# A recurrence with an expert layer behind it: the same steps issued in another order, with other transposes on the DMA queue

## The chip, the cores and the metric

The kernel runs on one core of a Trainium2 chip. The metric is the time of one execution on the device in microseconds (us); lower is better. The engines are named as the profile names them: PE is TensorE (PEld its weight loads), DVE is VectorE, ACT is ScalarE, POOL is GpSimd, and SP is SyncE, whose queue issues nearly all DMAs here. Each engine takes its instructions in the order in which they were issued to it, and an instruction that waits holds up all behind it.

## The reference

Thirty-two heads (batch 4, 8 heads) of width 40 carry a state over 768 steps; the outputs of all heads of a token form a row of 320, and a layer with 2048 hidden units follows. Cut to what matters:

```python
for t in range(S):
    y[:, :, t] = np.einsum('bhd,bhde->bhe', rt, state)
    Sa = np.einsum('bhde,bhe->bhd', state, at)
    state_decay = state * wt[:, :, None, :] - np.einsum('bhd,bhe->bhde', Sa, bt)
    state = state_decay + np.einsum('bhd,bhe->bhde', vt, kt)
...
x = attn_out.transpose(0, 2, 1, 3).reshape(B * S, H * D)
h = x @ w_in                      # 3072 x 320 @ 320 x 2048
g = np.maximum(h, 0.0) ** 2
return g @ w_out                  # 3072 x 2048 @ 2048 x 320
```

## The kernel before

The 768 steps are cut into 12 chunks of 64. Within a chunk the recurrence is written as matrix products over the chunk's steps, for 16 pairs of heads; from chunk to chunk only the state is handed on. The names of the steps carry the chunk's number `c`:

- Loads: `ldw`, `ldk`, `ldb`, `lda`, `ldr`, `ldv c` bring the six inputs into the tiles `raw_w`, `raw_kb`, `raw_a`, `raw_r`, `raw_v`, two buffers of each. A load is two DMAs of 160 KB (`ldw` four of 80 KB in chunks 0 to 3). `lwi`, `lwl` and `lwo` bring the expert weights, through tiles that later hold other data.
- Preparation: `ln` (logarithm of w, tile `lnW`), `hi` and `lo` (its two halves), `cf` and `ci` (running sums, on PE), `eg`, `ef`, `ec`, `ei`, `ex` (exponentials, tiles `iG`, `GT`, `Gin`), `castk`, `castb`, `castA`, `castR`, `castV` (to bf16) or `mulKB` (keys times `iG`, from chunk 4).
- Transposes on PE and their evictions: `Tk`, `Tb`, `TK` to `KBT`; `TA`, `TR` to `AR`; `TU` back from `KBT`; `TV` to `VUT`; `TS` to `Sb`; `XT` to `XT`. The eviction has the same name in small letters. A transpose is either narrow (two matmuls of 64 rows each per block) or wide (one matmul of 128 rows), as the table `WIDE` says.
- Transposing DMAs: for chunks in `TV_DMA`, `TS_DMA`, `TK_DMA` the transpose of V, of the state or of K is no step of PE but a DMA on SyncE's queue, `ldt`, `lds` or `ldz`.
- The chain from chunk to chunk: `EN` and `mEN` (products of keys, masked on DVE), `AS` (the old state's part), `EV`, `u0`, `NU`, `u1` (the corrected values, tile `VU`), `S` and `s` (the new state `STb`).
- The output of a chunk: `CX`, `mCX`, `RS`, `Y`, `y`, `yd`, `XT`, `xt`.
- The expert layer: `F` and `FL` (first product, units u0 to u3; `FL` is the last 64 rows of the input width), `f` (maximum with 0), `q` (square), `O` (second product; `OL` for chunk 11), `o` (eviction), `st` (store).
- `WD` steps are matmuls whose result nobody reads.

PE writes into four PSUM tiles `pb`, and a step that opens one names it (`PE2` is the third); it waits until what was there has been evicted.

A planner has written out what is issued when: its string `ORDER` names an engine and a step in each entry, and `Plan.issue` goes through it from first to last. A step can have several possible engines (copies may go to DVE, ACT or POOL), and the entry says which. The engines run by themselves after that, held only by data, buffers and semaphores. DMAs take eight semaphores in turn: a DMA can be issued only when the last one with the same semaphore has landed, so no more than eight are under way.

Of the kernel before, what the change touches and what calls it, by code (L numbers as in the profile page):

```python
# [88 lines left out]
1; DVE hi 0 h1; DVE zs 1; POOL zk 1; POOL castk 0; DVE lo 0 h1; PE cf 0 h1; ACT eg 0 h0; POOL
castb 0; ACT eg 0 h1; DVE zk 0; SP lda 0; PE1 Tk 0; DVE za 0; DVE tk 0 g1; DVE tk 0 g0; PE3 Tb 0;  # L90
DVE tb 0 g0; ACT ef 0; DVE tb 0 g1; PE2 ci 0 h0; PE ci 0 h1; POOL castA 0; PE0 TA 0; DVE tA 0 g1;
PE1 WD2; POOL zk 2; PE1 TU 0; SP ldw 1; ACT ln 1; ACT ec 0; DVE tA 0 g0; DVE tU 0; PE3 EN 0 g1;
DVE mEN 0 g1; POOL hi 1; SP ldk 1; PE0 EN 0 g0; POOL lo 1; ACT ldb 1; ACT castA 1; SP ldv 0; PE2
cf 1; PE1 TA 1; POOL castV 0 g1; ACT eg 1; POOL castV 0 g0; ACT ef 1; DVE mEN 0 g0; PE3 ci 1; ACT
ec 1; SP ldw 2; DVE tA 1 g1; PE0 EV 0; POOL castk 1; PE2 Tk 1; ACT u0 0; PE NU 0; ACT ln 2; DVE tA
1 g0; ACT u1 0 g0; ACT u1 0 g1; DVE tk 1 g0; DVE tk 1 g1; POOL castb 1; PE1 Tb 1; DVE tb 1 g0; SP
ldr 0; POOL castR 0; DVE tb 1 g1; PE3 TR 0; ACT tR 0 g1; POOL hi 2; ACT tR 0 g0; PE2 S 0 g0; PE S
0 g1; DVE s 0 q0; SP ldv 1; DVE s 0 q1; PE0 TV 0; ACT tV 0; POOL lo 2; ACT castV 1 g1; PE1 EN 1
g1; DVE mEN 1 g1; SP ldb 2; PE3 EN 1 g0; DVE mEN 1 g0; PE2 TU 1; ACT tU 1; PE0 CX 0 g1; DVE mCX 0
g1; PE1 cf 2; SP ldv 2; POOL zv 1; SP lda 2; PE3 CX 0 g0; PE2 AS 1; POOL castV 1 g0; PE EV 1; DVE  # L100
mCX 0 g0; POOL castb 2; PE0 Tb 2; ACT eg 2; POOL castA 2; DVE tb 2 g1; ACT u0 1; DVE tb 2 g0; PE3
TA 2; PE NU 1; ACT ef 2; DVE tA 2 g0; SP ldk 2; PE1 Y 0; DVE yd 0; DVE y 0; DVE tA 2 g1; SP ldr 1;
POOL castR 1; SP lwi 0 u1; POOL cwi 0 u1; ACT u1 1 g0; ACT u1 1 g1; PE0 SC 1; PE S 1 g0; SP lwi 0
u0; PE S 1 g1; DVE s 1 q0; ACT castk 2; PE1 XT 0; PE2 ci 2; ACT castV 2 g1; ACT xt 0; ACT ec 2;
PE3 Tk 2; DVE s 1 q1; PE1 TR 1; ACT tR 1 g0; ACT tR 1 g1; PE2 TV 1; DVE tk 2 g0; PE0 EN 2 g0; DVE
tk 2 g1; PE3 EN 2 g1; DVE mEN 2 g0; SP ldw 3; POOL castV 2 g0; ACT tV 1; POOL zv 2; ACT ln 3; POOL
hi 3; DVE mEN 2 g1; PE1 TU 2; SP lwl 0; DVE tU 2; POOL lo 3; PE0 TS 1; DVE tS 1; SP ldr 2; POOL
castR 2; SP ldk 3; SP ldb 3; PE2 AS 2; PE EV 2; PE3 TS 0; SP lwi 0 u2; PE1 CX 1 g1; DVE tS 0; ACT
u0 2; ACT cwl 0; PE NU 2; ACT u1 2 g0; DVE mCX 1 g1; PE0 CX 1 g0; DVE mCX 1 g0; ACT u1 2 g1; PE3
cf 3; ACT ef 3; PE1 SC 2; PE S 2 g0; PE S 2 g1; POOL castk 3; PE2 F 0 u1; PE0 Tk 3; DVE s 2 q1;  # L110
POOL cwi 0 u0; ACT eg 3; DVE s 2 q0; ACT castb 3; DVE tk 3 g0; SP lda 3; PE FL 0 u1; ACT f 0 u1;
DVE tk 3 g1; PE3 ci 3; ACT ec 3; SP ldv 3; PE1 RS 1; PE Y 1; PE2 TV 2; ACT tV 2; PE3 FL 0 u2; DVE
y 1; DVE yd 1; PE1 XT 1; PE0 Tb 3; DVE xt 1; DVE tb 3 g0; POOL cwi 0 u2; DVE tb 3 g1; PE F 0 u2;
ACT f 0 u2; POOL castA 3; PE1 TA 3; SP lwi 0 u3; PE2 TR 2; ACT tR 2 g0; ACT tR 2 g1; DVE tA 3 g0;
ACT castV 3 g1; DVE tA 3 g1; PE0 TS 2; POOL cwi 0 u3; PE3 F 1 u1; DVE tS 2; PE FL 1 u1; ACT f 1
u1; SP ldw 4; SP lwo 0 x3; POOL castV 3 g0; ACT ln 4; PE2 CX 2 g1; POOL cwo 0 x3; PE1 FL 0 u3; DVE
mCX 2 g1; SP ldb 4; PE0 EN 3 g1; POOL hi 4; POOL lo 4; SP ldr 3; POOL castR 3; PE F 0 u3; DVE mEN
3 g1; POOL q 1 u1; PE3 F 1 u0; PE2 EN 3 g0; DVE mEN 3 g0; ACT f 0 u3; PE0 CX 2 g0; DVE mCX 2 g0;
ACT q 0 u3; PE FL 1 u0; ACT f 1 u0; PE1 FL 1 u2; SP lwo 0 x0; POOL cwo 0 x0; PE F 1 u2; PE2 F 0
u0; PE FL 0 u0; DVE f 0 u0; POOL q 0 u0; PE3 ci 4 h0; ACT f 1 u2; SP lwo 0 x1; ACT ex 4 h0 g1; PE0  # L120
cf 4; PE1 AS 3; PE EV 3; POOL cwo 0 x1; DVE u0 3; ACT ef 4; PE2 RS 2; PE Y 2; ACT ei 4 h0; SP lda
4; ACT ex 4 h0 g0; SP lwo 0 x2; PE0 ci 4 h1; ACT ex 4 h1 g1; DVE y 2; POOL q 0 u1; PE NU 3; ACT ei
4 h1; ACT u1 3 g0; SP lwo 0 x5; POOL cwo 0 x5; PE3 FL 1 u3; DVE yd 2; PE2 TU 3; DVE tU 3; DVE u1 3
g1; SP lwo 0 x4; PE F 1 u3; ACT ex 4 h1 g0; PE0 TR 3; ACT castA 4; SP lwo 0 x6; PE2 TA 4; DVE tA 4
g0; DVE tA 4 g1; ACT f 1 u3; PE1 SC 3; PE S 3 g0; PE S 3 g1; DVE s 3 q0; DVE s 3 q1; PE3 TV 3; ACT
q 0 u2; SP ldw 5; SP lwo 0 x7; PE2 O 0 u0; ACT q 1 u0; DVE tR 3 g0; POOL cwo 0 x2; DVE tR 3 g1; PE
O 0 u1; ACT tV 3; PE1 CX 3 g0; ACT ln 5; ACT cwo 0 x7; PE3 TS 3; PE0 XT 2; ACT xt 2; POOL cwo 0
x6; DVE tS 3; DVE mCX 3 g0; POOL z 3; ACT k 3 q0; SP ldk 4; SP ldr 4; POOL cwo 0 x4; PE O 0 u2; PE
O 0 u3; DVE o 0; PE1 CX 3 g1; POOL hi 5; POOL lo 5; PE0 ci 5 h1; ACT q 1 u3; PE3 FL 2 u0; POOL
mulKB 4 h1; ACT ex 5 h1 g1; PE F 2 u0; POOL mulKB 4 h0; POOL q 1 u2; ACT ex 5 h1 g0; ACT ei 5 h1;  # L130
# [1067 lines left out]
```

## Time and profile before

| what | us |
| --- | --- |
| three runs | 236.6, 236.7, 237.03 |
| median | 236.7 |
| the profiled execution | 236.31 |
| its span, first to last instruction | 234.4 |

The granted TensorE clock was 0.993 of full speed over the span. The span can be read in three parts. Until the first expert product on PE the chunks 0 to 2 are loaded and prepared, and so are the expert weights. Then PE works on the recurrence and the expert layer in turn, and loads and transposing DMAs go on beside it. In the last part the recurrence is done and the expert products of chunks 10 and 11 follow each other.

In rows of the profile, `out<-in` are tiles of the kernel, `xN` is the number of instructions in a row, and what stands in brackets at the end is how long the engine was idle before it and what ended that.

### The profile page before, as it was taken

How to read it: one execution, taken by the hardware profiler on the slowest of the kernel's cores; microseconds unless marked ns; L12 is line 12 of the kernel's file. 1: busy time of each engine (PE TensorE's matmuls, PEld its weight loads, DVE VectorE, ACT ScalarE, POOL GpSimd, SP SyncE). 2: the span in 40 equal slices, each digit the busy share in tenths (PEclk: the TensorE clock that was granted, in tenths of full speed). 3: DMA queues.
4: the chain of work that ended last, by engine and by line, in shares of the span. 5: the costliest groups of instructions: out<-in, count | busy, mean ns of one | idle time of the engine just before them, and what ended most of it. 6: DMA issues, size and time to landing. Idle time of an engine off the chain costs nothing.

```text
span 234.4 us, 11927 instructions
## 1 busy us (share of the span) xinstructions
PE 221.3 (94%) x5367; PEld 172.0 (73%) x5367; DVE 179.4 (77%) x228; ACT 176.1 (75%) x235; POOL 141.6 (60%) x144
## 2 busy tenths in 40 slices
PE   8768979998999999999999999997999999999997
PEld 2558868786887677787788687775677877878873
DVE  5777999887687768978987878969689677758550
ACT  3467997978997969799888988986789933863631
POOL 7659326446999774379774959682296990320320
PEclk9997999999999999999999999999999999999999
DMA  6899697997997888887889799799999796811004
GB/s 167 230 193 196 187 243 196 239 184 163 312 213 148 158 156 203 160 151 156 196 179 178 152 171 174 145 183 167 195 120 175 154 165 142 170 37 47 12 6 108
DMA packets 115609, 38.26 MB, mean 163 GB/s; under 512 B 99690, under 2 KB 115558, under 8 KB 115558
## 3 DMA queue, kind: packets, MB, share of 16 engines
q1 hardware_dynamic: 114006, 36.19, 76.3%
q10 hardware_dynamic: 1552, 1.31, 2.0%
q8 instruction: 42, 0.69, 1.2%
q14 instruction: 9, 0.07, 0.1%
HBM read 28.84 MB, written 3.93 MB: 140 GB/s over the span
## 4 chain that ended last, share of the span: by engine, by line
PE 66%; DMA 13%; SPq 6%; ACT 5%; POOL 4%; issue 3%; DVE 2%; POOLq 0%; ACTq 0%; DVEq 0%
PE pb L391 37%; PE pb L987 22%; DMA G<-in_moe_w_in_dram 5%; PE pb L395 4%; DMA raw_w<-in_w_dram 3%; DMA VUT<-VU 2%; DMA raw_kb<-in_k_dram 2%; PE pb L399 2%; ACT G L1015 2%; SPq L434 2%; SPq L464 1%; SPq L1101 1%; PE pb L1153 1%; POOL WIN L381 1%; ACT Gin L670 1%
## 5 line engine op out<-in xcount | busy, mean ns | idle before, releaser
L1023 POOL TENSOR_TENSOR G<-G 128x1024 bf16<-128x1024 bf16 x25 | 47.2, 1893 | 29.0 <-DVE G L1017 14.6
L391 PE MATMUL pb<-WOUT,G 128*128 128x320 bf16 x384 | 56.2, 299 | 0.1
L987 PE MATMUL pb<-XT,WIN 128*128 128x256 bf16 x384 | 48.4, 273 | 0.5 <-ACT G L1015 0.3
L391 PEld LDWEIGHTS <-G 128*128 128x128 bf16 x384 | 36.3, 98 | 14.5 <-issue 0.7
L1015 ACT ACTIVATE G<-pb 128x1024 bf16<-128x1024 f32 x36 | 36.5, 1022 | 10.3 <-PE pb L987 9.0
L987 PEld LDWEIGHTS <-WIN 128*128 128x128 bf16 x384 | 34.9, 98 | 7.9 <-issue 3.2
L765 DVE TENSOR_TENSOR CX<-pb,UTI 128x1024 bf16<-128x1024 f32 x24 | 28.8, 1218 | 6.9 <-PE pb L391 5.2
L765 DVE TENSOR_TENSOR EN<-pb,MSK 128x1024 bf16<-128x1024 f32 x24 | 28.8, 1218 | 3.3 <-PE pb L391 3.0
L385 POOL TENSOR_TENSOR KB<-raw_kb,iG 128x640 bf16<-128x640 f32 x13 | 19.9, 1543 | 11.1 <-ACT iG L664 5.3
L1025 ACT ACTIVATE G<-G 128x1024 bf16<-128x1024 bf16 x19 | 19.8, 1054 | 3.5 <-DVE G L1017 3.3
L1017 DVE TENSOR_SCALAR G<-pb 128x1024 bf16<-128x1024 f32 x12 | 14.6, 1220 | 6.7 <-PE pb L987 5.1
L866 DVE TENSOR_TENSOR STb<-pb,GT 40x640 bf16<-40x640 f32 x22 | 18.1, 822 | 1.5 <-PE pb L391 1.1
L740 DVE TENSOR_TENSOR AR<-pb,GT 128x512 bf16<-128x512 bf16 x24 | 15.7, 683 | 4.1 <-PE pb L395 2.4
L987 PE MATMUL pb<-XT,WLAST 64*128 64x256 bf16 x192 | 17.2, 271 | 1.1 <-ACT G L1015 0.9
L391 PEld LDWEIGHTS <-EN 64*64 64x64 bf16 (+1 forms) x768 | 14.7, 111 | 3.7 <-issue 2.9
L385 POOL TENSOR_TENSOR lo<-lnW,hi 128x640 bf16<-128x640 f32 (+1 forms) x11 | 14.8, 1347 | 3.0 <-PE pb L391 2.3
L949 DVE TENSOR_TENSOR Yb<-pb,Gin 128x128 bf16<-128x128 f32 (+1 forms) x24 | 12.3, 549 | 3.3 <-PE pb L391 3.3
L670 ACT ACTIVATE Gin<-pb 64x320 f32<-64x320 f32 x32 | 13.7, 429 | 1.0 <-PE pb L391 0.4
L377 ACT ACTIVATE VU<-pb 64x640 bf16<-64x640 f32 x18 | 12.5, 696 | 1.8 <-issue 1.1
L377 ACT ACTIVATE VUT<-pb 128x2048 bf16<-128x2048 bf16 x6 | 11.2, 1874 | 2.7 <-PE pb L395 1.9
L377 ACT ACTIVATE osb<-pb 128x640 f32<-128x640 f32 (+1 forms) x8 | 5.1, 636 | 10.8 <-PE pb L391 10.8
L701 ACT ACTIVATE GT<-pb 128x1024 f32<-128x1024 f32 x12 | 12.3, 1021 | 0.7 <-PE pb L391 0.6
(127 smaller groups left out, 443.9 us busy)
## 6 DMA issues: line engine op xcount, KB each, us to landing
raw_kb<-in_k_dram SPq DMA_DIRECT2D x24, 160.0 KB, 4.3
raw_v<-in_v_dram SPq DMA_DIRECT2D x24, 160.0 KB, 4.8
raw_a<-in_a_dram SPq DMA_DIRECT2D x22, 160.0 KB, 3.2
raw_r<-in_r_dram SPq DMA_DIRECT2D x22, 160.0 KB, 4.5
out_dram<-osb SPq DMA_DIRECT2D x22, 160.0 KB, 2.7
raw_kb<-in_b_dram SPq DMA_DIRECT2D x20, 160.0 KB, 4.9
G<-in_moe_w_in_dram SPq DMA_DIRECT2D x10, 256.0 KB
raw_w<-in_w_dram SPq DMA_DIRECT2D x16, 160.0 KB, 5.1
```

The costliest lines, as they stand in the source:

```text
L377: alts.append(("ACT", c_act(n), lambda: nc.scalar.activation(out=o_(), in_=i_(), func=ACTF.Copy, scale=1.0 if scale is None else scale)))
L385: return [("POOL", 40 + 2.35 * n, lambda: nc.gpsimd.tensor_tensor(out=o_(), in0=a_(), in1=b_(), op=op)), ("DVE", c_dve(n), lambda: nc.vect ...
L391: return lambda: nc.tensor.matmul(out=o_(), lhsT=l_(), rhs=r_(), start=start, stop=stop, skip_group_check=True)
L670: nc.scalar.activation(out=Gin[c % NGI][rows(g), NP * jh:NP * jh + NP, :].rearrange("p j e -> p (j e)"), in_=slot(hb, FP32)[rows(g), g, 0: ...
L740: ew(f"tA {c} g{g}", [("DVE", c_dve(512), lambda g=g: nc.vector.tensor_tensor(out=steps(AR[q2][:, 0, g]), in0=turned(ha, g), in1=steps(GT[ ...
L765: ew(f"m{nm} {c} g{g}", [("DVE", c_dve(1024), lambda: nc.vector.tensor_tensor(out=dst[q2][:, g].rearrange("p q i t -> p (q i) t"), in0=slo ...
L866: ew(f"s {c} q{q}", [("DVE", c_dve(2 * n), lambda q=q: nc.vector.tensor_tensor(out=STb[q2][live(q), :, q, 0:D], in0=slot(hs, FP32)[live(q) ...
L987: return lambda: nc.tensor.matmul(out=o_(), lhsT=l_(), rhs=r_(), start=begins and opens(hf, x), stop=ends and not opens(hf, x), skip_group ...
L1015: ("ACT", c_act(1024), lambda gb=gb, hf=hf: nc.scalar.activation(out=gb, in_=slot(hf, FP32)[:], func=ACTF.Relu)),
L1017: ("DVE", c_dve(1024), lambda gb=gb, hf=hf: nc.vector.tensor_scalar(out=gb, in0=slot(hf, FP32)[:], scalar1=0.0, scalar2=None, op0=ALU.max))],
L1023: ("POOL", 1900, lambda gv=gv: nc.gpsimd.tensor_tensor(out=gv, in0=gv, in1=gv, op=ALU.mult)),
L1025: ("ACT", c_act(1024), lambda gv=gv: nc.scalar.activation(out=gv, in_=gv, func=ACTF.Square))],
```

## The change

The kernel's code stays, and so do the steps. The tables and the string `ORDER` change:

- `TV_DMA` loses chunk 8, `TS_DMA` gains chunk 5, `TK_DMA` gains chunk 9: nine transposing DMAs become ten, and PE has `TV 8` for `TS 5` and `TK 9`.
- `WIDE`: `Tk 1`, `Tb 2`, `Tk 3`, `TA 3`, `TR 3`, `TA 4`, `TR 8`, `TR 9`, `TV 2`, `TV 3` become narrow; `TA 0`, `TR 2`, `TR 6`, `TV 1` become wide. (`cf 4` and `cf 7` in it have no effect.)
- `ORDER` puts the steps into another order on all engines, and some 130 evictions, casts, squares and the like on another engine. `WD` steps: 2 at the start and 11 at the end before; 7 at the start and 8 at the end now. The expert products of chunk 0 and 1 begin in it ahead of most of chunk 3's steps.

```diff
-TV_DMA = (8, 9, 10, )
-TS_DMA = (6, 8, 9, 10, )
-TK_DMA = (10, 11, )
-WIDE = """TA 1; TA 3; TA 4; TR 0; TR 1; TR 3; TR 8; TR 9; TS 1; TU 0; TU 1; TU 2; TU 3; TV 2; TV 3; Tb 0;
-Tb 1; Tb 2; Tk 0; Tk 1; Tk 2; Tk 3"""
+TV_DMA = (9, 10, )
+TS_DMA = (5, 6, 8, 9, 10, )
+TK_DMA = (9, 10, 11, )
+WIDE = """TA 0; TA 1; TR 0; TR 1; TR 2; TR 6; TS 1; TU 0; TU 1; TU 2; TU 3; TV 1; Tb 0; Tb 1; Tk 0; Tk 2;
+cf 4; cf 7"""
...
-ORDER = """ACT ldw 0 h1; SP ldw 0 h0; DVE zs 0; DVE zr 0; ACT ldb 0; DVE zz 0; DVE zr 1; SP ldk 0; POOL za 1;
+ORDER = """POOL zv 0; DVE zk 1; SP ldw 0 h0; POOL zr 0; DVE zs 1; DVE zr 1; ACT ldw 0 h1; DVE zs 0; ACT ldk 1;
...
```

Three places show what moves. In the rows the line numbers are those of each kernel (the new one's code stands three lines higher), and a number behind a tile's name tells its buffer.

ScalarE in the first third of the start, before: `ln 1`, the load b 1 (`raw_kb_68`), then the preparation of chunk 1, `u0 0` (`NZ`), `ln 2` (`lnW` from `raw_w_65`) and `u1 0` (`VU`).

```order
L615 ACTIVATE lnW_75<-raw_w_66 128x640
L647 ACTIVATE Gin_79<-pb_151 128x640
L449 DMA raw_kb_68<-in_b_dram 128x1x320 x2
L377 ACTIVATE tA_91<-raw_a_70 128x2x8x40
L566 ACTIVATE iG_78<-pb_151 128x1024
L701 ACTIVATE GT_83<-pb_151 128x16x64
L647 ACTIVATE Gin_80<-pb_152 128x640
L377 ACTIVATE NZ_94<-pb_149 128x640
L615 ACTIVATE lnW_75<-raw_w_65 128x640
L377 ACTIVATE VU_87<-pb_149 64x16x40 x2
```

The same stretch now:

```order
L612 ACTIVATE lnW_75<-raw_w_66 128x640 [waits DMAHW5_49,DMAHW6_49,DMAHW2_49,DMAHW7_49,DVE_49,Activation_49]
L461 DMA raw_a_70<-in_a_dram 128x1x320
L461 DMA raw_a_70<-in_a_dram 128x1x320 [waits DMAHW3_49]
L446 DMA raw_kb_67<-in_k_dram 128x1x320 [waits DMAHW4_49,DMAHW0_49,Pool_49]
L446 DMA raw_kb_67<-in_k_dram 128x1x320 [waits DMAHW1_49]
L644 ACTIVATE Gin_80<-pb_150 128x640 [waits PE_49]
L563 ACTIVATE iG_78<-pb_151 128x1024 [waits DVE_49,PE_49,Activation_49]
L698 ACTIVATE GT_83<-pb_151 128x16x64
L374 ACTIVATE NZ_94<-pb_152 128x640 [waits DVE_49,PE_49]
L612 ACTIVATE lnW_75<-raw_w_65 128x640 [waits DMAHW1_49,DMAHW2_49,DMAHW0_49,DMAHW3_49,Activation_49,Pool_49]
L374 ACTIVATE VU_87<-pb_152 64x16x40 [waits PE_49]
```

The loads a 1 (`raw_a_70`) and k 2 (`raw_kb_67`) now stand on ScalarE's queue behind `ln 1`, and the load of a 0 and of k 1 ahead of it; `ln 2` still stands between `u0 0` and `u1 0`.

SyncE's queue from the load w 2 (`raw_w_65`, four DMAs) to v 1 (`raw_v_74`), before, with what each DMA waits for:

```order
L434 DMA raw_w_65<-in_w_dram 32x8x80 [waits DMAHW6_49,Activation_49]
L434 DMA raw_w_65<-in_w_dram 32x8x80 [waits DMAHW7_49,DMAHW3_49]
L434 DMA raw_w_65<-in_w_dram 32x8x80 [waits DMAHW0_49]
L434 DMA raw_w_65<-in_w_dram 32x8x80 [waits DMAHW1_49]
L474 DMA raw_r_71<-in_r_dram 128x1x320 [waits DMAHW2_49]
L474 DMA raw_r_71<-in_r_dram 128x1x320 [waits DMAHW3_49]
L458 DMA raw_v_74<-in_v_dram 64x16x40 [waits DMAHW4_49]
L458 DMA raw_v_74<-in_v_dram 64x16x40 [waits DMAHW5_49]
```

And now:

```order
L431 DMA raw_w_65<-in_w_dram 32x8x80 [waits DMAHW0_49,Activation_49]
L431 DMA raw_w_65<-in_w_dram 32x8x80 [waits DMAHW3_49,DMAHW1_49]
L431 DMA raw_w_65<-in_w_dram 32x8x80 [waits DMAHW2_49]
L431 DMA raw_w_65<-in_w_dram 32x8x80 [waits DMAHW3_49]
L471 DMA raw_r_71<-in_r_dram 128x1x320 [waits DMAHW4_49]
L471 DMA raw_r_71<-in_r_dram 128x1x320 [waits DMAHW5_49]
L455 DMA raw_v_74<-in_v_dram 64x16x40 [waits DMAHW6_49]
L455 DMA raw_v_74<-in_v_dram 64x16x40 [waits DMAHW7_49]
```

The rows are the same; what stands behind the semaphores is not. In the new program the semaphores 2 and 3 belong to the load a 1 at that point, and 4 and 5 to the load k 2, both on ScalarE's queue; the third and fourth DMA of w 2 and the load r 0 wait for those.

SyncE's queue near two thirds of the program, where a transposing DMA was late before:

```order
L452 DMA raw_kb0_67<-in_k_dram 64x16x40 x2
L1058 DMA out_0_dram<-osb0_115 64x2x320 x2
L458 DMA raw_v1_74<-in_v_dram 64x16x40 x2
L909 DMA_TRANSPOSE VUT0_97<-VU2_89 128x16x128
L464 DMA raw_a0_69<-in_a_dram 128x1x320 x2
L885 DMA_TRANSPOSE Sb0_107<-STb0_105 128x16x128
```

And now:

```order
L1055 DMA out_0_dram<-osb0_115 64x2x320 x2
L435 DMA raw_w1_66<-in_w_dram 64x16x40 x2
L538 DMA_TRANSPOSE KBT1_96<-KB0_84 128x16x128
L449 DMA raw_kb0_67<-in_k_dram 64x16x40 x2
L461 DMA raw_a0_69<-in_a_dram 128x1x320 x2
L1055 DMA out_0_dram<-osb0_115 64x2x320 x2
```

`ldt 8` (to `VUT`) is gone, since `TV 8` is a step of PE now, and `ldz 9` (to `KBT`) stands near its place.

More of the change, by code (lines that the diff above doesn't have):

```diff
@@ L89 @@
[L89 to L130, printed above, removed]
```

217 lines of the change are left out of this document (128 added, 89 removed).

## The prediction

> **What bounds the kernel now.** I read the page first, then the waits of TensorE, then stretches of 5 us, and last the order of time on ScalarE's, SyncE's and TensorE's own queues. The page says that PE is busy nearly throughout:
>
> ```profile
> span 234.4 us, 11927 instructions
> ...
> PE 221.3 (94%) x5367; PEld 172.0 (73%) x5367; DVE 179.4 (77%) x228; ACT 176.1 (75%) x235; POOL 141.6 (60%) x144
> ```
>
> The chain of waits has PE's first expert product at 43 us; from there to 230 us PE's waits for others are nearly one single wait:
>
> ```profile
> 43.19 0.98 PE pb L987 x8
> ```
>
> ```profile
> PE pb L391 <- DMA VUT<-VU: 2.0, 1, 2.0
> PE pb L987 <- ACT G L1015: 1.2, 2, 0.9
> ```
>
> So after 43 us an order can gain through PE's own work, through that 2.0 us, and through short handoffs of a PSUM bank. Ahead of 43 us it is different. Three stretches (busy time of each engine, granted clock, DMA share, GB/s):
>
> ```profile
> 5.00:10.00 5.00, 4.05 (x54) 2.44 (x53) 2.83 (x7) 2.13 (x6) 3.79 (x6) 1.00 0.96 259
> 15.00:20.00 5.00, 3.34 (x101) 2.65 (x96) 2.81 (x4) 3.78 (x5) 3.38 (x5) 1.00 0.87 178
> 20.00:25.00 5.00, 4.86 (x139) 4.56 (x132) 4.46 (x7) 4.05 (x6) 4.33 (x6) 0.66 0.86 179
> ```
>
> No compute engine is full from 15 to 20 us, while the DMA engines are at 0.87: the start runs at the pace of the loads, and their order decides.
>
> **The change part by part.** *The start.* The loads of k 1 and k 2 go out on ScalarE's queue, a 0 too, and b 0 and b 1 go to SyncE's. The rows on which this rests, ScalarE first, then SyncE:
>
> ```profile
> 11.34 0.74 ACT L615 ACTIVATE lnW<-raw_w 128x640 f32<-128x640 f32 x1 [1.11 <-DVE KBT L584]
> 11.39 1.20 ACTq L449 DMA_DIRECT2D raw_kb<-in_b_dram  x2
> ...
> 19.36 0.73 ACT L615 ACTIVATE lnW<-raw_w 128x640 f32<-128x640 f32 x1
> 20.23 1.42 ACT L377 ACTIVATE VU<-pb 64x640 bf16<-64x640 f32 x2
> 21.89 1.08 ACT L377 ACTIVATE AR<-pb 128x512 bf16<-128x512 bf16 x2 [0.24 <-PE pb L399]
> 23.51 1.88 ACT L377 ACTIVATE VUT<-pb 128x2048 bf16<-128x2048 bf16 x1 [0.54 <-PE pb L395]
> ...
> 27.03 1.01 ACT L566 ACTIVATE iG<-pb 128x1024 f32<-128x1024 f32 x1
> 28.37 0.70 ACT L377 ACTIVATE NZ<-pb 128x640 bf16<-128x640 f32 x1 [0.33 <-PE pb L391]
> ```
>
> ```profile
> 11.47 3.52 SPq L434 DMA_DIRECT2D raw_w<-in_w_dram  x4
> 15.04 1.75 SPq L474 DMA_DIRECT2D raw_r<-in_r_dram  x2
> ```
>
> From issue to landing, raw_a and then raw_w in the first 30 us (minimum, median, maximum):
>
> ```profile
> DMA to landing us min/median/max: 4.9/4.9/4.9
> ```
>
> ```profile
> DMA to landing us min/median/max: 4.1/5.9/7.6
> ```
>
> In the old order w 2 goes out between 11.47 and 15.0. In the new one its third and fourth DMA wait for the semaphores of a 1, and a 1 goes out on ScalarE behind `ln 1`: at 12.1 (11.34 + 0.74) the first, some 0.6 later the second. With 4.9 that lands at 17.6, the last part of w 2 goes out then, and with the median of 5.9 it lands at 23.5 (21.7 to 25.2 by the ends). `ln 2` (19.36 before) waits for it, and behind `ln 2` on ScalarE now stand `u1 0`, `tV 0`, two `tR 0`, `ef 2`, `eg 2` and `u0 1`. By the rows above: `ln 2` 23.5 to 24.2, `u1 0` (1.42) to 25.7, `TV 0` and `tV 0` (1.88) to 28.4, `tR 0` 1.08, `ef 2` and `eg 2` 1.01 each to 31.6, `u0 1` to 32.3 instead of 29.07 (28.37 + 0.70). Chunk 1's recurrence is then 3.1 us late (1.4 by the lowest landing, 4.9 by the highest). r 0 is late too, since it waits for k 2, but it needs no more than this. PE has nothing to put there: behind `NU 0` stand only `TU 1` and `EN 1 g1` before it needs `u1 0`. How much of 3.1 survives to the first expert product the trace can't show: later loads hold both orders. The ends are 0 and 4.9; I take 2.8, near the worked value, because PE's lost time is not made up where PE is the bound. **+2.8.**
>
> [...]
>
> *Wide and narrow transposes.* PE's rows, the start of the next row being the end of a step's share of PE:
>
> ```profile
> 49.28 0.61 PE L399 MATMUL pb<-IDQ,tA 128*128 128x128 bf16 x8
> 49.83 0.41 PE L395 MATMUL pb<-IDQ,tR 64*128 64x64 bf16 x16
> 50.08 0.57 PE L395 MATMUL pb<-IDQ,STb 40*128 40x40 bf16 x32
> ...
> 66.44 1.07 PE L399 MATMUL pb<-IDQ,VU 128*128 128x128 bf16 x16
> 67.34 0.43 PE L391 MATMUL pb<-WOUT,G 128*128 128x320 bf16 x2
> ...
> 88.15 0.63 PE L395 MATMUL pb<-IDQ,VU 64*128 64x64 bf16 x32
> 88.61 0.40 PE L395 MATMUL pb<-IDQ,tR 64*128 64x64 bf16 x16
> ```
>
> Eight wide matmuls take 0.55, the sixteen narrow 0.25: 0.30 saved by each of eight steps that become narrow, lost by each of three that become wide: 5 x 0.30 = 1.5. `TV 2` and `TV 3` become narrow, `TV 1` wide: 0.90 against 0.46, so 0.44. `TS 5` (0.5, the third row) leaves PE; `TK 9` leaves and `TV 8` comes, which cancels (both 32 narrow matmuls). Nearly all lies behind 43 us, where PE is the bound: **-2.4.** The evictions of these steps stay, beside PE.
>
> *The wait for VUT.* `TV 8` on PE takes the place of the DMA that made PE wait:
>
> ```profile
> 162.22 0.41 PE L391 MATMUL pb<-AR,KBT 64*128 64x64 bf16 x16
> 164.58 0.41 PE L391 MATMUL pb<-AR,VUT 64*128 64x64 bf16 x16 [1.95 <-DMA VUT<-VU]
> ```
>
> **-2.0.** What is late next: the transposing DMA `ldz 9` stands on SyncE at the same place, and `EN 9 g1` needs it. SyncE's queue there:
>
> ```profile
> 153.05 1.33 SPq L452 DMA_DIRECT2D raw_kb<-in_k_dram  x2
> 154.48 2.70 SPq L1058 DMA_DIRECT2D out_dram<-osb  x2
> ...
> 158.84 3.70 SPq L909 DMA_TRANSPOSE VUT<-VU  x1
> ...
> 163.93 2.41 SPq L885 DMA_TRANSPOSE Sb<-STb  x1
> ```
>
> `ldz 9` has the place on SyncE that the row of 154.48 had; ahead of it stands one `Sb` transpose more (2.41) and one load less (1.33), so it starts near 155.6. The row of 158.84 needed 5.7 until PE went on (164.58), so `KBT` is there near 161.3, and PE comes to it near 162 (the row of 162.22, as much work done). Ends: 0, and +3 if SyncE is 3 us later; I take **+0.6**, near the computed arrival.
>
> *Handoffs of banks.* The new order sets some consumers closer behind their producers. `TV 2` now stands behind `NU 2`, `ci 3`, `RS 1`, `Y 1`, and needs both `u1 2`, one behind the other:
>
> ```profile
> 60.62 0.46 PE L391 MATMUL pb<-Sb,AR 128*64 128x80 bf16 x16
> 60.91 0.66 PE L391 MATMUL pb<-KB,CX 128*64 128x40 bf16 x32
> ...
> 61.88 0.68 PE L391 MATMUL pb<-NZ,EN 64*64 64x40 bf16 x32
> ```
>
> ```profile
> 204.64 0.82 DVE L374 TENSOR_SCALAR VU<-pb 64x640 bf16<-64x640 f32 x1 [0.39 <-PE pb L391]
> ...
> 205.54 0.70 ACT L377 ACTIVATE VU<-pb 64x640 bf16<-64x640 f32 x1 [0.83 <-issue]
> ```
>
> From `NU`'s start the chain takes 0.68 + 0.70 + 0.82 = 2.2, PE's work meanwhile 0.6 + 0.3 + 0.3 + 0.6 = 1.8: PE waits 0.4. Taken so over all PE steps, with the durations of such rows, the new order is short by 8.6 us at 46 places and the old by 5.0 at 30. Neighbouring places share one wait, so of the difference of 3.6 (the upper end; the lower is 0) I take half: **+1.8.**
>
> *At no cost.* Three of the eleven fills at the end move to the start, where PE waits anyway. At the end they hid behind the last store, by these rows:
>
> ```profile
> out_dram<-osb SPq DMA_DIRECT2D x22, 160.0 KB, 2.7
> ```
>
> ```profile
> 230.48 2.54 PE L1153 MATMUL pb<-UTI 128*128 128x512 bf16 x11
> 231.15 0.30 ACTq L1067 DMA_DIRECT2D out_dram<-osb  x1
> ```
>
> The fills end at 233.0, the store at 231.15 + 2.7 = 233.9. The other evictions change engines in both directions; the engines they go to have as much free time as those they leave.
>
> **The sum.** 2.8 - 2.4 - 2.0 + 0.6 + 1.8 = +0.8 on the profiled execution's 236.3 (span 234.4 and 1.9 around it), so 237.1; the median of the runs shown is 0.4 above the profiled one: 237.5.
>
> **The rivals.** *Faster: the late start does not count.* If the loads that come after it (w 3, the first expert weights) hold PE as long in both orders, the 2.8 falls away and 234.7 is left. For it: the DMA share of 0.86 and more all through the start. Against it: the recurrence itself is what is late, and PE's work behind it is not shortened. It decides where less than 2.0 of the 2.8 survives. *Slower: `ldz 9` is late.* Each us that SyncE comes later to it is a us of PE's time; at 3 us, 240.5. For it: SyncE issues without a pause there. Against it: most loads ahead of it are early ones. *Slower: a second stretch at half clock.* The row of 20 to 25 us shows 0.66, which is 3.4 us at half. Between `NU 0` and `TV 0` PE would now have 1.5 us of work in some 5 us (`TU 1` by this row, `EN` by that of 162.22):
>
> ```profile
> 24.26 1.05 PE L399 MATMUL pb<-IDQ,KBT 128*128 128x128 bf16 x16
> ```
>
> One more such stretch makes up to 3.4 us of work last twice as long, so +1.7: 239.2. [...] *The order does not matter.* DMA and PE are both near full, the two gains and the two losses cancel: 236.7. For it: the total work hardly changes. Against it: each single term is larger than what cancels.
>
> **How the numbers follow.** Forecast 0.42; late start absorbed 0.33; `ldz 9` late 0.10; half clock 0.07; no effect 0.08. Under 0.2% (0.5 us) a measurement of this kernel can't tell from no change. The forecast's own range, 236 to 239, lies above +0.5 us with 0.33, within with 0.07, below with 0.02; the absorbed start is faster with 0.31, within with 0.02; "no effect" divides 0.05 within, 0.03 faster; the two other rivals are slower. Faster 0.36, within 0.14, slower 0.50. The range reaches to both sides' rivals: 234.3 (start absorbed, half of the handoffs hidden too) to 241.0 (`ldz 9` late on top of the forecast).
>
> **What would show it.** The logarithm of chunk 2 (`lnW`, third 128x640 row) starts near 23.5 instead of 19.4 with raw_w as what ended the wait, and `u1 0` behind it; PE's wait for `VUT` is gone, and one for `KBT` near 160 is under 1 us; PE's busy work is 2 us less; more short waits for evictions from 50 to 150 us. If the third `lnW` row starts before 21, the first term is wrong and the kernel is faster; a wait for `KBT` or `Sb` over 2 us makes it slower than said.

## The result

The changed kernel is slower: 242.5 us at the median against 236.65 us, 1.027 times the time before (95% interval 1.021 to 1.033). Run a second time on another chip it was 1.031 (1.027 to 1.036). In this text medians are over all runs of a kernel, ratios leave out runs more than 1.5% above its fastest, and where the two differ the ratio is the one to go by. The forecast was 237.5 us, and its range ended at 241.0.

The profiled execution took 240.7 us, 4.4 us more than the one of before. Its page (the span, the engines, and the queue that carries instructions) and TensorE's waits from 43 us to the end, as waiter, what it waited for, total, times and longest:

```profile
span 239.0 us, 11976 instructions
...
PE 221.0 (92%) x5393; PEld 168.8 (71%) x5393; DVE 177.6 (74%) x230; ACT 172.0 (72%) x227; POOL 148.6 (62%) x150
...
q8 instruction: 42, 0.69, 1.2%
```

```profile
PE pb L388 <- issue: 5.1, 5, 1.9
PE pb L392 <- DVE STb L863: 0.7, 2, 0.5
PE pb L388 <- DVE EN L762: 0.6, 2, 0.3
PE pb L984 <- ACT KBT L374: 0.3, 1, 0.3
PE pb L984 <- issue: 0.2, 1, 0.2
PE pb L388 <- DVE CX L762: 0.2, 1, 0.2
```

The wait of 2.0 for `VUT` is gone, `ldz 9` makes nobody wait, and waits for evictions are small. In their place stands a wait that the prediction did not know: 5.1 us in which PE waits for "issue", that is, for nothing that the profile shows. It comes in the middle of steps whose inputs are all there. TensorE's order of time at the three places where it is longest, ahead of and behind the gap (start, duration, what, and in brackets the idle time before it):

```profile
45.04 0.57 PE L388 MATMUL pb<-KB,CX 128*64 128x40 bf16 x26
47.06 0.27 PE L388 MATMUL pb<-KB,CX 128*64 128x40 bf16 x6 [1.45 <-issue]
...
62.73 0.44 PE L388 MATMUL pb<-VU,EN 128*64 128x40 bf16 x18
63.92 0.40 PE L388 MATMUL pb<-VU,EN 128*64 128x40 bf16 x14 [0.74 <-issue]
```

```profile
155.09 0.52 PE L388 MATMUL pb<-NZ,EN 64*64 64x40 bf16 x21
157.47 0.36 PE L388 MATMUL pb<-NZ,EN 64*64 64x40 bf16 x11 [1.85 <-issue]
```

The last is `NU 8`: 21 of its 32 matmuls run, PE stands still for 1.85 us, and the other eleven run. Three stretches of before and after (busy time of PE, PEld, DVE, ACT, POOL, then granted clock, DMA share, GB/s) show where this falls, before first:

```profile
45.00:50.00 5.00, 5.00 (x135) 4.34 (x136) 3.83 (x8) 4.03 (x5) 1.76 (x2) 1.00 0.95 182
50.00:55.00 5.00, 4.90 (x128) 3.88 (x122) 4.31 (x6) 3.49 (x6) 2.32 (x3) 1.00 0.98 204
155.00:160.00 5.00, 5.00 (x139) 3.89 (x137) 3.90 (x6) 4.46 (x6) 4.13 (x4) 1.00 0.85 163
```

```profile
45.00:50.00 5.00, 3.55 (x92) 2.62 (x88) 2.90 (x4) 1.99 (x3) 0.72 (x1) 0.74 0.84 173
50.00:55.00 5.00, 4.79 (x111) 3.87 (x108) 4.12 (x6) 4.10 (x7) 3.54 (x3) 0.91 0.94 248
155.00:160.00 5.00, 3.15 (x52) 2.16 (x48) 2.77 (x5) 2.87 (x5) 1.08 (x2) 1.00 0.85 185
```

PE's busy time falls to 3.55 and 3.15 of 5 us there. The first place also shows a granted clock of 0.74 and 0.91: the half-clock stretch (in both traces 3.41 us at a granted clock of 0.50), which before began at 20.34 us, in the start, begins at 47.45 us now, 0.4 us behind the gap of 1.45 and among the expert products.

What the gaps have in common is found by counting TensorE's instructions (each matmul is two, with its weight load: 5393 of each on the page). The places lie 188 to 190 instructions past a multiple of 256, and 42 transfers of 16 KB on the instruction queue (0.69 MB, the row above) go with the 10,786 instructions: 256 in each. The trace has the time of each transfer. For five blocks of the changed kernel and one of before, in us:

```
kernel   block   began at   transfer of the next block   next block begins   behind the transfer
after      7       41.68        44.00 - 45.81                47.06               1.25
after     10       58.27        60.61 - 62.40                63.91               1.51
after     29      152.90       155.17 - 156.13              157.47               1.34
after     13       72.75        74.25 - 75.21                79.51               4.30  (no gap)
after     22      118.85       119.60 - 120.59              121.96               1.37  (no gap over 0.25)
before    29      149.10       149.59 - 151.19              153.94               2.75  (no gap)
```

The next block's transfer starts only after the block before it has begun (0.2 to 2.8 us later in nearly all blocks), takes 0.9 to 1.8 us, and no block begins earlier than 1.2 us behind its transfer's end (the first 24 us left out). So most blocks last 4 us or more, even where their matmuls need less; the shortest here, block 22, lasted 3.1 us, its transfer having started 0.75 us after it began. Block 29 holds `AS 8`, `EV 8`, `cf 9`, `TA 9`, `ci 9 h0` and most of `NU 8`: some 2.5 us of work. The next one, with the two `O 5` in it, lasts 6.5 us. I call these gaps waits for code. Taken from one matmul's start to the next one's (2.04 us where the row says 1.85), and counted where they are over 0.25 us, lie at a block's limit and end within 1.85 us of a transfer, after 24 us, they are 8.2 us in 8 places in the profiled execution of after, and 2.3 us in 3 of before.

### The profile page after: what moved, and what is told of

Read it like the earlier page. It is cut to its first block, busy times and chain, and to the rows that moved or that the text cites. A ratio compares the mean times of both kernels' runs of the same rounds, so it can differ in the third digit from the quotient of the medians.

```text
span 239.0 us, 11976 instructions
## 1 busy us (share of the span) xinstructions
PE 221.0 (92%) x5393; PEld 168.8 (71%) x5393; DVE 177.6 (74%) x230; ACT 172.0 (72%) x227; POOL 148.6 (62%) x150
## 4 chain that ended last, share of the span: by engine, by line
PE 67%; DMA 12%; issue 6%; DVE 4%; POOL 3%; SPq 3%; ACT 2%; ACTq 1%; POOLq 0%; DVEq 0%
PE pb L388 40%; PE pb L984 20%; PE pb L392 6%; DMA raw_v<-in_v_dram 4%; DMA raw_kb<-in_k_dram 4%; DMA raw_kb<-in_b_dram 2%; DMA raw_a<-in_a_dram 2%; SPq L1098 2%; DVE STb L863 1%; ACT G L1012 1%; POOL G L1020 1%; POOL WIN L378 1%; DVE EN L762 1%; PE pb L1150 1%; DVE pb L859 1%
## 5 line engine op out<-in xcount | busy, mean ns | idle before, releaser
L1020 POOL TENSOR_TENSOR G<-G 128x1024 bf16<-128x1024 bf16 x27 | 52.0, 1934 | 34.5 <-DVE G L1014 14.6
L1012 ACT ACTIVATE G<-pb 128x1024 bf16<-128x1024 f32 x41 | 41.7, 1024 | 13.7 <-PE pb L984 12.5
L984 PE MATMUL pb<-XT,WIN 128*128 128x256 bf16 x384 | 48.9, 274 | 0.7 <-ACT KBT L374 0.3
L382 POOL TENSOR_TENSOR lo<-lnW,hi 128x640 bf16<-128x640 f32 x10 | 14.0, 1401 | 6.9 <-DVE hi L369 5.1
L374 ACT ACTIVATE VU<-pb 64x640 bf16<-64x640 f32 x16 | 11.2, 698 | 7.1 <-PE pb L388 4.1
L946 DVE TENSOR_TENSOR Yb<-pb,Gin 128x640 bf16<-128x640 f32 (+1 forms) x24 | 12.4, 550 | 5.3 <-PE pb L388 4.8
L1022 ACT ACTIVATE G<-G 128x1024 bf16<-128x1024 bf16 x14 | 14.6, 1053 | 0.1
L378 POOL CAST hi<-lnW 128x640 bf16<-128x640 f32 x8 | 5.8, 721 | 13.2 <-ACT lnW L612 7.5
L661 ACT ACTIVATE iG<-pb 128x640 f32<-128x640 f32 x16 | 11.1, 696 | 2.7 <-PE pb L388 2.3
L374 ACT ACTIVATE osb<-pb 128x640 f32<-128x640 f32 (+1 forms) x11 | 7.2, 654 | 8.0 <-PE pb L388 7.9
```

The source lines that it names most:

```text
L374: alts.append(("ACT", c_act(n), lambda: nc.scalar.activation(out=o_(), in_=i_(), func=ACTF.Copy, scale=1.0 if scale is None else scale)))
L382: return [("POOL", 40 + 2.35 * n, lambda: nc.gpsimd.tensor_tensor(out=o_(), in0=a_(), in1=b_(), op=op)), ("DVE", c_dve(n), lambda: nc.vect ...
L984: return lambda: nc.tensor.matmul(out=o_(), lhsT=l_(), rhs=r_(), start=begins and opens(hf, x), stop=ends and not opens(hf, x), skip_group ...
L1012: ("ACT", c_act(1024), lambda gb=gb, hf=hf: nc.scalar.activation(out=gb, in_=slot(hf, FP32)[:], func=ACTF.Relu)),
L1020: ("POOL", 1900, lambda gv=gv: nc.gpsimd.tensor_tensor(out=gv, in0=gv, in1=gv, op=ALU.mult)),
L1022: ("ACT", c_act(1024), lambda gv=gv: nc.scalar.activation(out=gv, in_=gv, func=ACTF.Square))],
```

## The experiments

Theory A: the work in a block of 128 matmuls decides; a block of less than some 4 us makes TensorE wait for code. Rival B: the order of loads and bank handoffs, as the prediction had it. Rival C: half-clock stretches as a cause of their own. For theory A I counted what an order would cost from its steps' matmuls and their shares of TensorE (0.02 to 0.135 us a matmul): each block from the fifth on (some 30 us on) as its work or 4.1 us, whichever is more (4.1 is an estimate from the two traces, where most blocks last 4 us or more). What the blocks fall short of 4.1 us comes to some 6 us more in the changed kernel than in the one before. It is an estimate, since single blocks can be shorter.

**Moving the limits of the blocks without moving a step.** Tiny matmuls, whose result nobody reads, are put behind the 14 that open the program. 72 of them in the kernel before:

```diff
                              lhsT=ones[:], rhs=rhs, start=True, stop=True, skip_group_check=True)
+        for j in range(72):
+            nc.tensor.matmul(out=banks[0][rows(j % 2), 0, 0:64], lhsT=ones[rows(j % 2), rows(j % 2)],
+                             rhs=ones[rows(j % 2), 0:64], start=True, stop=True, skip_group_check=True)
```

> The kernel before, with 72 tiny matmuls (64x64 by 64x64, result read by nobody) behind the 14 that open the program, where TensorE waits for its first data: no step changes its place in the order. Theory A (TensorE's instructions come in blocks of 256, and a block that is worked off in less than about 4 us makes TensorE wait for the code of the next): the 144 instructions shift every block limit, other steps share a block, and by the work in each block (0.02 to 0.2 us a matmul) what is short of 3.8 to 4.2 us per block grows from 4 to 9 us to 13 to 20: slower by 7 to 11 us. Rival B (what counts is the order of loads and of bank handoffs, as the prediction had it): within 0.5 us of before, since TensorE waits there anyway. Rival C (half-clock stretches make the difference): within 1.7 us.

Measured: 244.7 us against 235.9 at the medians, and 1.029 (1.023 to 1.035) by the ratio, which is some 7 us, at the lower end of what was expected. The profiled execution was the longest of them, 248.0 us. Its waits of PE from 12 to 232 us have:

```profile
PE pb L389 <- issue: 8.6, 6, 3.1
PE pb L393 <- issue: 1.8, 2, 1.1
PE pb L397 <- issue: 0.7, 1, 0.7
PE pb L985 <- issue: 0.4, 1, 0.4
```

11.5 us, where the kernel before has 1.6 in its execution of 236.3 (two rows, of 1.3 and 0.3). No step was moved, only the blocks' limits, and the time rose by about as much as by the change itself. Theory A had this; B had it within 0.5 us and C within 1.7.

With a whole block of 128, the limits fall on the old steps again:

```diff
+        for j in range(128):
```

> The kernel before with 128 tiny matmuls at its start instead of 72, which is 256 instructions, one block more exactly: every later block holds the same steps as in the kernel before. Theory A: 0 to 1 us slower than before, where 72 cost 8.8. Rival (the extra matmuls themselves cost, in whatever block): at least what 72 cost, 9 us or more.

Measured: 235.2 against 236.4 (0.996, 0.992 to 1.001). 72 matmuls cost some 7 us, 128 nothing. It isn't the matmuls, it is where the limits fall.

Now 104 in the changed kernel, and the same 104 in the kernel before:

```diff
+        for j in range(104):
```

> The changed kernel with 104 such tiny matmuls at its start. Theory A: by the same count the best place of the block limits for this order; what is short falls by 3.5 to 3.9 us, so 238.5 to 239.5 where the changed kernel has 242. Rival B: no change, within 0.5 us. Rival C: no change in the mean, within 1.7 us.

> The kernel before with the 104 tiny matmuls at its start that made the changed kernel 4.6 us faster. Theory A (code blocks): for this order it is a poor place of the block limits; what is short of 3.8 us a block is 10.3 us against 4.5 without them: slower by 4 to 7 us, 240 to 243. Rival C (tiny matmuls at the start help by keeping TensorE busy): as fast as before or faster.

Measured: the changed kernel 237.9 against 235.9 (1.006, 1.002 to 1.011), where it had 1.027 and 1.031 without them: some 5 us gained. The kernel before with the same 104: 238.6 against 235.25 (1.013, 1.008 to 1.017), a loss of 3.0 to 3.4 us, its sign as expected and its size under the lower end of 4. A thing that is good for one order and bad for the other is not a matter of a busier TensorE at the start. The profile of the changed kernel with 104 has four rows of "issue" of 0.5 to 0.7, the largest:

```profile
PE pb L397 <- issue: 0.7, 1, 0.7
```

Two more places of the limits in the changed kernel, 56 and 104 + 128 = 232:

```diff
+        for j in range(56):
```

```diff
+        for j in range(232):
```

> The changed kernel with 56 tiny matmuls at its start instead of 104. Theory A (code blocks): the worst place of the block limits for this order; what is short grows by 2.2 us against the changed kernel without them, so 243 to 246. Rival C (the tiny matmuls help because they keep TensorE busy at the start, so that the clock isn't halved): more than half of the gain of 104, 239 to 240. Rival B (order of loads and bank handoffs): 242, as the changed kernel.

> The changed kernel with 232 tiny matmuls at its start: 104 and one whole block of 128 more. Theory A: the same block limits as with 104, so 237 to 239 (237.9 with 104). If the number of tiny matmuls counts and not the place of the limits: another time, 240 or more.

Both missed. With 56 the kernel took 240.6 against 236.4 (1.018, 1.011 to 1.025), if anything faster than the changed kernel without them, where the count had it slower; its profile still has 9.0 us of waits for code. Why is open. With 232 it took 243.6 against 235.25 at the medians (1.024, 1.018 to 1.030). Here the traces say why: the block pattern is that of 104 (4.3 us of waits for code against 3.9; from the end of block 5 to that of block 41 it takes 177.6 us, with 104 from block 4 to block 40 it takes 177.2), but block 5 with 232 ends at 32.6 where block 4 with 104 ends at 29.3. The loss is at the very start, which I had taken to be idle: 246 matmuls that need two blocks of code hold TensorE while the first data wait for it. TensorE's rows with 232, from the tiny matmuls to the first step of the program, and that first step in the changed kernel:

```profile
5.92 3.51 PE L1163 MATMUL pb<-ones 64*64 64x64 bf16 x209
11.29 0.78 PE L1163 MATMUL pb<-ones 64*64 64x64 bf16 x23 [1.87 <-issue]
12.00 0.39 PE L389 MATMUL pb<-UT,hi 64*128 64x128 bf16 x4
```

```profile
6.89 0.28 PE L388 MATMUL pb<-UT,hi 64*128 64x128 bf16 x4
```

The first step begins at 12.00 instead of 6.89, and by the clock of 0.66 a half-clock stretch lies there too. The stretch from 10 to 15 us, with 232 and, behind it, in the changed kernel (DVE does nothing, the third number behind the comma):

```profile
10.00:15.00 5.00, 3.49 (x71) 3.16 (x70) 0.00 (x0) 0.80 (x3) 0.72 (x1) 0.66 0.75 154
```

```profile
10.00:15.00 5.00, 4.46 (x83) 3.42 (x83) 4.82 (x8) 1.83 (x3) 3.50 (x4) 1.00 0.97 211
```

**The same place of the limits with fewer matmuls.** Two early transposes are made wide. This takes 24 matmuls out by 23 us, and since 104 + 24 = 128, every later limit falls where it falls with 104 added:

```diff
-WIDE = """TA 0; TA 1; TR 0; TR 1; TR 2; TR 6; TS 1; TU 0; TU 1; TU 2; TU 3; TV 1; Tb 0; Tb 1; Tk 0; Tk 2;
-cf 4; cf 7"""
+WIDE = """TA 0; TA 1; TR 0; TR 1; TR 2; TR 6; TS 1; TU 0; TU 1; TU 2; TU 3; TV 1; Tb 0; Tb 1; Tk 0; Tk 2;
+cf 4; cf 7; TV 0; Tk 1"""
```

> The changed kernel with two early transposes wide (TV 0 and Tk 1): 24 matmuls fewer by 23 us, 0.7 us more work on TensorE. Every later block limit falls on the same steps as with the 104 tiny matmuls (104 + 24 = 128), with no matmul added. Counting each block of 128 matmuls from the fifth on as its work or 4.1 us, whichever is more, gives 4.0 us less than the changed kernel. Theory A (code blocks): 237.5 to 239.5. Rival C (tiny matmuls help by keeping TensorE busy at the start): 242.5 to 243.5, since nothing is added and the work grows.

Measured: 237.2 against 235.7 (1.005, 1.001 to 1.009). Two words in a table take back some 5 of the 6 us, with 0.7 us of work more. Nothing is added here that could keep TensorE busy, and the steps stand in the changed order; what is left as a cause is where the limits fall. Not all waits for code are gone: the profiled execution, of 238.2 us, has 5.6 us of them, 2.2 in one place at 49 us. The stretch of `NU 8`, of the changed kernel and with the two wide transposes:

```profile
152.00:160.00 8.00, 6.15 (x186) 4.66 (x183) 5.46 (x7) 5.31 (x9) 4.08 (x3) 1.00 0.89 191
```

```profile
152.00:160.00 8.00, 8.00 (x245) 6.21 (x243) 6.95 (x9) 6.53 (x12) 5.39 (x5) 1.00 0.95 184
```

**What a block costs by itself.** 384 tiny matmuls (three blocks, `WT384`) near 109 us, and 384 behind the last work, where no data moves (a DMA share of 0.01 from 243 to 252 us):

```diff
-PE2 O 3 u0;
+PE2 WT384; PE2 O 3 u0;
...
-PE0 WD8
+PE0 WD8; PE0 WT384
```

> The kernel before with 384 tiny matmuls (768 instructions, three blocks) ahead of O 3 u0 near 109 us and 384 more behind its last work, where no data moves. Theory A: TensorE can do such a matmul in 0.02 us, 7.7 us for 384, but is held by the code: about 4 us per 128 near 109 us (12 us for 384), and 3 us per 128 at the end, where no other DMA is under way (9 us). Rival (no limit by code): 7.7 us or less at both places.

TensorE's order of time, at the first and then at the second place:

```profile
108.31 0.88 PE L1149 MATMUL pb<-UTI 64*64 64x64 bf16 x44
110.57 2.21 PE L1149 MATMUL pb<-UTI 64*64 64x64 bf16 x128 [1.38 <-issue]
114.58 2.21 PE L1149 MATMUL pb<-UTI 64*64 64x64 bf16 x128 [1.79 <-issue]
118.85 1.33 PE L1149 MATMUL pb<-UTI 64*64 64x64 bf16 x73 [2.07 <-issue]
```

```profile
242.81 3.82 PE L1149 MATMUL pb<-UTI 64*64 64x64 bf16 x229
247.39 2.21 PE L1149 MATMUL pb<-UTI 64*64 64x64 bf16 x128 [0.75 <-issue]
251.11 0.63 PE L1149 MATMUL pb<-UTI 64*64 64x64 bf16 x27 [1.52 <-issue]
```

The pieces are 128 long: one block. A block begins every 4.0 to 4.3 us (110.57, 114.58, 118.85) for 2.2 us of work, and 3.7 us lie between two (247.39 to 251.11) with no other traffic. The 3 us expected at the end was too little: most of the time of a block is not due to traffic. This is one execution, and the blocks here are short ones behind short ones.

**Less traffic.** From chunk 4 on, only the first DMA of each load of w, k, b, v and a is kept:

```diff
-                for g in range(2):
+                for g in range(1):
                     q_.dma_start(
                         out=raw_kb[c % NKBR][rows(g if nm == "b" else 1 - g),
...
-            for g in range(0 if c in BY8 else 2):
+            for g in range(0 if c in BY8 else 1):
...
-            for g in range(2):
+            for g in range(2 if c in BY8 else 1):
                 q_.dma_start(out=raw_v[c % NV][rows(1 - g)], in_=half(v, g))
...
-            for q in range(2):
+            for q in range(2 if c in BY8 else 1):
                 q_.dma_start(out=raw_a[c % NA][:, q, :], in_=xv[q])
```

> The changed kernel, from chunk 4 on with only the first of the two DMAs of each load of w, k, b, v and a (the second half of each tile keeps an earlier chunk's values, so later outputs differ). If the code of a block comes late because its DMA queues behind the data: the median time from a block's beginning to the start of its successor's transfer (1.65 us) falls towards 1 us, waits for code behind 80 us shrink to a half or less of their 4 us, and the time falls by 2 to 3 us. If the time to fetch a block is fixed whatever the traffic: those waits stay, and the time falls by less than 1 us.

Measured: 240.9 against 236.4 (1.016, 1.008 to 1.024), so 2.5 to 3.5 us less than the changed kernel by the ratios, though its interval overlaps with that of 1.027. But the reason isn't the one expected: the median time from a block's beginning to the start of the next transfer fell only by some 0.3 us, from 1.5 to 1.2, and the waits for code behind 80 us stayed at 3.9 us. What the smaller loads gained lies elsewhere and wasn't followed up.

**Spreading one dense block by hand.** In the changed kernel the two expert products `O 5 u0` and `u1` go ahead of `cf 9`, `TA 9`, `ci 9 h0` and `NU 8` (and `castA 9`, `q 5 u1`, `q 5 u0` ahead of them in the text, their order on their engines unchanged); three of the steps take other banks for it:

```diff
-PE3 cf 9; ... PE1 TA 9; ... PE2 ci 9 h0; ... PE NU 8; ... PE3 O 5 u0; PE O 5 u1;
+PE3 O 5 u0; PE O 5 u1; PE1 cf 9; ... PE2 TA 9; ... PE1 ci 9 h0; ... PE NU 8;
```

> The changed kernel with two expert products of chunk 5 (O 5 u0, u1, 1.08 us each) moved ahead of cf 9, TA 9, ci 9 h0 and NU 8 on TensorE; the block in which TensorE waited 2.04 us in the middle of NU 8 then holds 4.1 us of work instead of 2.3. Theory A: that wait goes, 1 to 2 us faster than the changed kernel. Rival B: NU 8 is 2.2 us later in the chain and TA 9 and ci 9 h0 wait for banks: no change or up to 1 us slower. Rival C: no change.

Measured: 243.9 against 235.9 (1.033, 1.029 to 1.038): no gain on the changed kernel. The wait for code in `NU 8` is gone, as theory A had it, but TensorE waits at the same place for evictions, as rival B had it (its waits from 150 to 165 us):

```profile
PE pb L389 <- DVE AR L738: 1.6, 1, 1.6
PE pb L389 <- ACT GT L699: 0.9, 1, 0.9
```

2.5 us of these for 1.85 of the other. A block is better spread where it costs no bank.

**The wait for VUT.** In the kernel before, `ldt 8` is issued ahead of a store:

```diff
-SP st 4; ... SP ldv 11; ... SP ldt 8;
+SP ldt 8; SP st 4; ... SP ldv 11;
```

> The kernel before with one entry moved: the transposing DMA ldt 8 (to VUT) is issued ahead of the store of chunk 4 instead of behind it and behind a load. If the wait of 1.95 us for VUT costs what it shows: 2.0 us faster than before (234.7). If something else takes its place (the code of the next block, the store's buffer): 0 to 1 us.

Measured: 235.8 against 235.9 at the medians; the ratio is 0.993 (0.988 to 0.998), a gain of 0.5 to 2.8 us. So the times don't decide between the two expectations. The profile has no wait for `VUT`, but 5.5 us of "issue" where the kernel before has 1.6, in an execution of 236.5. Other profiles say more: the kernel before with 72, 104 or 128 tiny matmuls has the same order on SyncE, and TensorE has no wait of 0.3 us or more for `VUT` in any of the three. With 128, SyncE's rows are:

```profile
151.56 2.47 SPq L1056 DMA_DIRECT2D out_dram<-osb  x2
154.13 1.47 SPq L456 DMA_DIRECT2D raw_v<-in_v_dram  x2
156.07 3.30 SPq L907 DMA_TRANSPOSE VUT<-VU  x1
```

`ldt 8` goes out at 156.07 there and at 158.84 in the prediction's profile. The wait of 1.95 us was that of one execution.

The move and a whole block of tiny matmuls together:

```diff
-SP st 4; ... SP ldv 11; ... SP ldt 8;
+SP ldt 8; SP st 4; ... SP ldv 11;
...
+        for j in range(128):
```

> The kernel before with ldt 8 issued ahead of the store of chunk 4 and 128 tiny matmuls (one whole block) at its start. If the wait for VUT costs what it shows and the block limits stay where they are: 1.5 to 2 us faster than before. If the transposing DMA ahead of a store and a load delays the fetches of code or other loads by as much: no change.

Measured: 237.1 against 235.25 (1.009, 1.006 to 1.013), a miss; its profile has 4.9 us of waits for code, three of them (2.6 us) behind 80 us, where the kernel with 128 alone has one. Why is open. The gain of `ldt 8` alone is not confirmed by it.

**The changed kernel once more**, with no edit, for its time beside others:

> The changed kernel as it is, for its time beside the others on one chip: 242 (2.7% above before).

Measured: 242.9 against 235.25 (1.031, 1.027 to 1.036), with 10.6 us of waits for code in its profile, that of an execution of 246.3 us. The mean granted clock over its executions is 0.979 (0.982 without its two longest); the kernel before had 0.994 on the same chip. The traces of before and of after have one half-clock stretch of 3.41 us each, and a mean of 0.993 and 0.992, so one lowers the mean by some 0.007 (half of 3.41 in some 237 us); by this estimate the changed kernel has two to three per execution and the kernel before about one. With the two wide transposes the mean is 0.996.

**Choosing by the count alone.** Ten transposes are switched in each kernel, picked by the count of blocks and nothing else:

```diff
 changed kernel
-TA 0; TA 1; TU 1; Tb 0
+TA 2; TA 4; TS 0; TS 4; TV 2; Tb 3
 kernel before
-TA 1; TA 4; TU 1; TV 3; Tb 0
+TA 7; TR 4; TR 7; TS 0; TV 1
```

> The changed kernel, its order kept, with ten transposes switched between narrow and wide (TA 0, TA 1, TU 1, Tb 0 narrow; TA 2, TA 4, TS 0, TS 4, TV 2, Tb 3 wide), chosen only by that count: 7.0 us less than the changed kernel, though TensorE has about 1.3 us more work. Theory A: 235 to 237.5, near the kernel before or under it. If the work of the steps decides and the limits don't: 243 to 244.

> The kernel before with ten transposes switched (TA 1, TA 4, TU 1, TV 3, Tb 0 narrow; TA 7, TR 4, TR 7, TS 0, TV 1 wide), chosen by the same count, which gives 2.2 us less than before. Theory A: 1 to 2.5 us faster than before. If the count is too rough for so small a difference: no change, or a loss at the start, where the count isn't valid.

Measured: the changed kernel 237.4 against 235.7 (1.0045, 1.000 to 1.009), some 5 us better for 7.0 counted, with some 0.9 us of work more (1.3 was said too high) and 2.4 us of waits for code in its profile. The kernel before 236.8 against 235.7 (1.001, 0.996 to 1.006): no change for 2.2 counted. The count finds gains of 5 us and is too rough for 2. Only `ldt 8` moved has an interval under 1, and with 128 tiny matmuls beside it the same move had 1.009: no kernel here beats the one before beyond doubt.

## Why the prediction was wrong

The sum was 2.8 - 2.4 - 2.0 + 0.6 + 1.8 = +0.8, and the time rose by 5.8 us. That both are "slower" is luck: the largest term that made it so came out as a gain. Term by term:

**The late start, +2.8: wrong.** The rows of ScalarE and SyncE in the changed kernel:

```profile
11.27 0.74 ACT L612 ACTIVATE lnW<-raw_w 128x640 f32<-128x640 f32 x1 [0.17 <-DMA raw_w<-in_w_dram]
11.28 1.20 ACTq L461 DMA_DIRECT2D raw_a<-in_a_dram  x2
...
18.76 0.73 ACT L612 ACTIVATE lnW<-raw_w 128x640 f32<-128x640 f32 x1
20.22 1.42 ACT L374 ACTIVATE VU<-pb 64x640 bf16<-64x640 f32 x2 [0.73 <-PE pb L388]
...
27.89 0.70 ACT L374 ACTIVATE NZ<-pb 128x640 bf16<-128x640 f32 x1 [0.77 <-PE pb L388]
```

```profile
12.10 4.53 SPq L431 DMA_DIRECT2D raw_w<-in_w_dram  x4
```

`ln 2` starts at 18.76 and not at 23.5. The chain named was there: the four DMAs of w 2 are out at 16.63 (12.10 + 4.53), 1.6 later than before (11.47 + 3.52). But a 1 was issued at 11.28, beside `ln 1` and not at 12.1 behind it, as the rows of before had shown (11.39 beside 11.34); and w 2's last part was there 2.1 us after 16.63 at the latest, where I had taken the load's median of 5.9. (By its own figures the chain was 3.2 us late, 32.3 against 29.07, and not 3.1.) `u0 1` is at 27.89 (before 28.37) and the first expert product at 42.49:

```profile
42.49 1.05 PE L984 MATMUL pb<-XT,WIN 128*128 128x256 bf16 x8
```

This is 0.6 sooner than before, though the steps ahead of it aren't all the same:

```profile
43.12 1.05 PE L987 MATMUL pb<-XT,WIN 128*128 128x256 bf16 x8
```

The rival "the late start does not count" was right in this, but gave 234.7.

**Narrow for wide, -2.4: right for the single step, wrong as a gain.** A narrow transpose does take 0.3 us less, as the rows said. It is also 8 or 16 matmuls more, and in a block that is held to 4.1 us each matmul costs 4.1/128 = 0.032 us: 8 of them are 0.26. By this estimate the saving in dense blocks is nearly nil, and every later limit moves. `TV 0` and `Tk 1`, made wide, cost 0.7 us of work and gained 5 us. PE's busy time on the page is 0.3 us less in the changed kernel (221.0 against 221.3), where the prediction had 2.

**The wait for VUT, -2.0, and `ldz 9`, +0.6.** The wait went, but it was no property of the kernel before: with its queue unchanged it was absent from three other profiles. `ldz 9` cost nothing here; TensorE's waits show no DMA to `KBT`.

**Handoffs, +1.8: too high.** The waits of PE for evictions from 43 us on sum to 1.8 us (0.7 + 0.6 + 0.3 + 0.2), those before to 1.4, so +0.4.

**What was missing: the code of the instructions.** The step that failed is "So after 43 us an order can gain through PE's own work, through that 2.0 us, and through short handoffs of a PSUM bank". It put waits for code at nothing, without a reason. A fourth thing was there to be read: the page's row of the instruction queue, and one "issue" wait of 1.3 us at 32 us, in the views of before:

```profile
q8 instruction: 42, 0.69, 1.2%
```

```profile
PE pb L391 <- issue: 1.3, 1, 1.3
```

Waits for code rose from 2.3 to 8.2 us in the two profiled executions, +5.9; the difference of their times is 4.4. The runs with shifted limits show that it is where the limits fall that decides. The sum of the waits in one execution is a poor measure of it: with the limits of the kernel before it is 2.3 us here, 4.5 with 128 tiny matmuls, 4.9 and 6.8 with `ldt 8` moved (with and without these), in executions of 234.8 to 236.5 us, and the changed kernel had 8.2 and 10.6 in its two.

**The second half-clock stretch, 239.2 with a chance of 0.07,** came nearer than the chance said: in the changed kernel the stretches are more, and one lies where TensorE is the bound. In the profiles they begin 0.4 to 2.2 us behind the end of a wait for code in the changed kernel (47.4) and in the kernel before with 72 (42.8 and 70.1); since moving the limits takes them away as well, they seem to go with these waits. Not all do: with `O 5` moved one begins at 18.8, and a wait of 2.0 us at 49 us, with the two wide transposes, has none behind it. That little work on PE brings such a stretch on was an assumption of the prediction, and no run shows it: from 155 to 160 us of the changed kernel PE is busy for 3.15 of 5 us, at a granted clock of 1.00. How much of the 6 us is clock and how much is code was not separated. An estimate of the most that the clock can be: one to two stretches more per execution, each costing at most half of its 3.41 us, are 1.7 to 3.4 us.

## What to carry to other kernels

Where a kernel issues thousands of short instructions on one engine, count them: here 128 short matmuls in a row took 3.7 to 4.3 us for 2.2 us of work, and the shortest block of the changed kernel took 3.1 us, so a run of short matmuls belongs between long ones. An edit that adds or removes a few matmuls early moves the limits of all later blocks, and its effect was 3 to 7 us here with no step moved; before an order is blamed or praised, shift it by half a block and by a whole one. A wait of one profiled execution is a term of a sum only if a second execution shows it.
